# A delta-rule attention and MoE kernel: another hand-written order for all its blocks, and three small edits

## The chip, the cores and the metric

The kernel runs on one core of a Trainium2 chip. The metric is the device time of one execution in microseconds (us); the time before is the median of three runs. Engines are named as in the profile: PE is TensorE (matmuls and transposes), DVE is VectorE, ACT is ScalarE, POOL is GpSimd and SP is SyncE, which here only issues transfers.

## The reference

Two parts follow each other. The first is a recurrence with a 48x48 state for each of 32 heads over 768 time steps; the second is a feed-forward layer on its output, 3072 tokens of 384 numbers.

```
k_n = k / (norm(k) + 1e-6)
for t in range(768):
    y[t]  = q[t] @ state
    v_old = k_n[t] @ state
    state = state + beta[t] * outer(k_n[t], v[t] - v_old)
x = y as (3072, 384)
h = x @ w_in                       # 384 x 2048
g = h * tanh(log(1 + exp(h)))      # the function Mish
out = g @ w_out                    # 2048 x 384
```

The weights come as 64-bit floats, which the kernel reads as pairs of 32-bit integers.

## The kernel before, in words

The 768 steps are cut into 12 chunks, n = 0 to 11, of 64 steps. The 32 heads lie as 16 pairs on 128 partitions, and most work on a chunk is done in two halves of 8 pairs, h = 0 and 1. A chunk is 256 rows of the feed-forward layer.

**The attention of a chunk.** `s_pg` (in the first chunks `early`) multiplies keys with keys into `pg` on PE. From `pg` DVE takes the part `d` (in `early` by `out`, L1436, otherwise by `gram_out`, L1386), and ACT the part `at`. `early(g)` does two chunks, 2g and 2g+1, at once: DVE transposes `d` into `gt` (L1456), norms are made, and a triangular system is solved column by column on DVE, in alternating instructions `pr` (L1504) and `gt` (L1506), 28 of them for g=0 and 60 for every later g. The solution is transposed back (`tu` and `tt` for g=0, L1517 and L1519; `d`, L1526, for later g). For g=0 `merge` joins two halves of the solution on PE (`ma`, `mb`; DVE adds `mb` at L1578 and transposes `tn`, L1580, and POOL moves a part, L1551). Then the stages of a chunk run on PE: `s_a` (tile `ta`), `s_b` (`tb`), `s_gq` (`gq`), `s_z` (`pz`), `s_y` (`py`, the output) and `s_s` (`ps`, the new state, which DVE adds at L1826 or ACT copies). The result `py` is split in a high part (ACT, L1786) and a low part (DVE, L1787) of `x`.

**The feed-forward layer.** `g1` does 18 matmuls 128x256 into `h` (L1883), since each product is a sum of three: high by high, low by high, high by low. There are 8 such blocks for each chunk. ACT makes `e` = Mish(h) and the high part of `g` (L1898, L1899), DVE the low part (L1900). `g2` adds 12 matmuls 128x384 into `acc` (L1917) for each block.

**The weights.** `convert` (L1279) makes a high and a low 32-bit part of each 64-bit weight, for 12 tiles `wi` of 128x512 and 16 tiles `wo` of 128x384: two to three DVE instructions (L1286, L1299, L1303), one or two on ACT, and the low part through PE (the tiles `loi` and `loo`) or through an adding transfer that POOL issues. This conversion lies between the solve of g=0 and some 20 us behind the first product.

**Filler.** `keep_warm` (L1941) puts matmuls 128x512 on a tile of zeros, `warm`, where PE would have no work. Their result is never used.

**What sets the order.** All five engines run in the order in which the program issues the instructions. Each piece of work is put on a heap with a rank (`put`), and `run` issues the pieces by rank. The table `TT` (L35) holds the rank of each piece, one number for each of its steps, so it is an order of all blocks on all engines and of the transfers on SP's queue. The table `SLOT` (L976) says which buffer of its pool a tile takes; each buffer makes the next writer wait for the last reader of the tile before.

## Time and profile before

| | |
|---|---|
| median of 3 runs | 598.23 us (597.74 to 598.76) |
| the profiled execution: its own time, its span | 597.18 us, 595.3 us |
| PE busy | 569.1 us, 96% of the span |
| DVE, ACT, POOL busy | 402.3, 273.8, 84.5 us |

Busy time says little here by itself: PE is busy 96% of the span, but in the first third another engine often decides when its next block may start. So the profile is read by stages. A stage is a stretch between two events, such as the start of one of DVE's transposes of `d`, and within it one compares PE's busy time with DVE's. The timeline gives the time at which an instruction starts, its duration, and in brackets how long its engine stood idle before it and for whom.

### The profile page before, as it was taken

The page shows a single profiled execution, that of the slowest core. Times are in us where ns is not written, and L with a number is a line of the kernel's source. Part 1 is how long each engine was busy: PE and PEld are TensorE (multiplying, and loading weights), DVE is VectorE, ACT ScalarE, POOL GpSimd, SP SyncE. Part 2 cuts the span into 40 slices and gives each one's busy share as a digit, 9 for nine tenths or more (in the row PEclk, how much of TensorE's full clock was granted, in tenths as well). Part 3 has the DMA queues.
Part 4 walks back from the last instruction along what each step waited for, and adds up shares of the span by engine and source line. Part 5 has one row for each costly group of instructions (what it writes and reads, how often), then busy time and mean ns, then how long its engine had stood idle before and what let it go on. Part 6 is the DMA issues. An engine that isn't in the chain of part 4 may idle for free.

```text
span 595.3 us, 22731 instructions
## 1 busy us (share of the span) xinstructions
PE 569.1 (96%) x9970; PEld 531.9 (89%) x9976; DVE 402.3 (68%) x877; ACT 273.8 (46%) x538; POOL 84.5 (14%) x148
## 2 busy tenths in 40 slices
PE   8589999999999999989999999999999999999997
PEld 5256889998998999989998999999999999999997
DVE  2898879999998658996468985569875424421210
ACT  4268886647333464316345324444343544332341
POOL 6010142224102202011101011210020101000000
PEclk9977999999999999999999999999999999999999
DMA  8998994732413435122424033312312203110011
GB/s 187 334 305 217 152 151 77 124 56 55 64 15 70 69 51 91 16 41 41 67 42 83 16 59 56 43 38 48 52 29 31 30 9 75 28 30 0 1 28 26
DMA packets 161778, 43.25 MB, mean 73 GB/s; under 512 B 149008, under 2 KB 157664, under 8 KB 161680
## 3 DMA queue, kind: packets, MB, share of 16 engines
q1 hardware_dynamic: 156640, 36.93, 31.1%
q0 software_dynamic: 2784, 4.29, 4.3%
q8 instruction: 78, 1.28, 0.9%
q10 hardware_dynamic: 2256, 0.59, 0.5%
q14 instruction: 20, 0.16, 0.1%
HBM read 32.87 MB, written 4.72 MB: 63 GB/s over the span
## 4 chain that ended last, share of the span: by engine, by line
PE 68%; DVE 9%; ACT 1%; issue 1%; POOL 0%; DVEq 0%; ACTq 0%
PE acc L1917 29%; PE h L1883 26%; PE py L1636 3%; PE pz L1636 3%; PE gq L1636 2%; DVE pr L1504 2%; DVE gt L1506 2%; PE pg L1636 1%; PE ps L1636 1%; DVE d L1526 1%; PE tb L1661 1%; PE ta L1661 1%; DVE g L1900 1%; DVE gt L1508 1%; DVE xx L1826 1%
## 5 line engine op out<-in xcount | busy, mean ns | idle before, releaser
L1883 PE MATMUL h<-x,wi 128*128 128x256 f32 x1728 | 212.2, 279 | 1.9 <-ACT e L1898 1.0
L1917 PE MATMUL acc<-wo,g 128*128 128x384 f32 x1152 | 212.2, 337 | 1.8 <-ACT g L1899 1.8
L1883 PEld LDWEIGHTS h<-x,wi 128*128 128x128 f32 x1728 | 204.2, 188 | 4.7 <-ACT e L1898 1.4
L1917 PEld LDWEIGHTS acc<-wo,g 128*128 128x128 f32 x1152 | 197.9, 188 | 4.3 <-ACT g L1899 2.1
L1900 DVE TENSOR_TENSOR g<-e,g 128x512 fp32r<-128x512 f32 x96 | 66.7, 700 | 84.1 <-ACT g L1899 83.4
L1898 ACT ACTIVATE e<-h 128x512 f32<-128x512 f32 x96 | 57.1, 598 | 126.8 <-PE h L1883 99.5
L1899 ACT CAST g<-e 128x512 fp32r<-128x512 f32 x96 | 58.8, 620 | 37.4 <-PE acc L1917 31.1
L1506 DVE TENSOR_TENSOR gt<-gt,pr 128x58 f32<-128x58 f32 (+9 forms) x164 | 58.5, 357 | 4.9
L1504 DVE TENSOR_TENSOR pr<-gt 128x58 f32<-128x58 f32 (+9 forms) x164 | 55.5, 339 | 4.2
L1636 PE MATMUL gq<-xx,kt 48*64 48x112 f32 (+1 forms) x768 | 49.3, 266 | 1.6 <-DVE d L1440 1.0
L1636 PEld LDWEIGHTS pz<-vt,tt 64*64 64x64 f32 x768 | 44.2, 139 | 5.7 <-issue 4.2
L1636 PE MATMUL pz<-vt,tt 64*64 64x48 f32 x768 | 47.7, 229 | 0.0
L1636 PEld LDWEIGHTS gq<-xx,kt 48*64 48x64 f32 x768 | 43.5, 132 | 2.7 <-DVE d L1440 1.1
L1765 ACT COPY xx<-pz 64x384 f32<-64x384 f32 x48 | 22.7, 474 | 43.0 <-PE gq L1636 26.4
L1740 DVE TENSOR_TENSOR xx<-gq,amask 64x256 f32<-64x256 f32 x96 | 40.2, 418 | 0.7
L1614 POOL TENSOR_TENSOR vt<-vt,ne 128x384 f32<-128x384 f32 x24 | 21.7, 910 | 132.8 <-DMA vt<-in_v_dram 118.9
L1545 POOL COPY tt<-d 32x512 f32<-32x512 f32 x40 | 25.9, 647 | 96.5 <-PE pz L1636 56.8
L1737 DVE TENSOR_TENSOR vt<-vt,gq 128x192 f32<-128x192 f32 x44 | 15.4, 351 | 29.1 <-PE tb L1661 9.0
L1621 DVE STREAM_TRANSPOSE xx<-xx 128x1024 f32<-128x1024 f32 x20 | 24.8, 1240 | 6.6 <-DMA xx<-in_q_dram 6.0
L1636 PE MATMUL py<-xx 128*32 128x64 f32 (+1 forms) x1536 | 26.6, 222 | 0.7 <-ACT xx L1765 0.7
L1636 PEld LDWEIGHTS py<-xx 128*32 128x32 f32 (+1 forms) x1536 | 22.6, 108 | 4.7 <-ACT xx L1765 1.4
L1826 DVE TENSOR_TENSOR xx<-xx,ps 48x384 f32<-48x384 f32 (+1 forms) x34 | 16.8, 494 | 7.7 <-PE pg L1636 3.4
(163 smaller groups left out, 608.0 us busy)
## 6 DMA issues: line engine op xcount, KB each, us to landing
...
```

The costliest lines, as they stand in the source:

```text
L1504: nc.vector.tensor_tensor(out=pv, in0=nj, in1=xj, op=ALU.mult)
L1506: nc.vector.tensor_tensor(out=below, in0=below, in1=pv, op=ALU.add)
L1545: nc.gpsimd.tensor_copy(out=tt2[r, t2, :, c0:c0 + 32], in_=dts[g][r, t2])
L1621: nc.vector.transpose(x, x)
L1636: last[:] = [nc.tensor.matmul(*a, start=True, stop=True)]
L1740: nc.vector.tensor_tensor(out=x[r, p4, hh, D:D + C], in0=ps[r, :, d:], in1=bcast_mid(amask[r], 4), op=ALU.mult)
L1826: nc.vector.tensor_tensor(out=old, in0=old, in1=(pt if q.start else ps)[src, q], op=ALU.add)
L1883: nc.tensor.matmul(h[:, f2, :], wt["i", f * P // WI * NCH + c][:, i2, f0:f0 + P], x[:, c, :], start=(i == 0), stop=(i == 3 * NCH - 1))
L1898: for d, f in ((0.7, lambda: nc.scalar.activation(e, h, AF.Mish)), (0.7, lambda: nc.scalar.copy(out=gg[:, 0], in_=e)), (0.8, lambda: nc.ve ...
L1899: (0.7, lambda: nc.scalar.copy(out=gg[:, 0], in_=e)),
L1900: (0.8, lambda: nc.vector.tensor_tensor(out=gg[:, 1], in0=e, in1=gg[:, 0], op=ALU.subtract))):
L1917: nc.tensor.matmul(acc[t], gg[:, a, f2, t * P:(t + 1) * P], wt["o", f][:, i2, :], start=(f == 0 and a == i2 == 0), stop=(f == NF - 1 and a ...
```

## The change

There are five parts.

1. `TT` is replaced: other ranks for all pieces, and so another order on every engine and of the 454 transfers on SP's queue. Nothing is added to or taken from the attention, the products or the conversions by this. `SLOT` is replaced with it.
2. The list of the fillers grows from 27 to 37 entries, and their matmuls from 53 to 71.
3. `unit` writes four blocks of the identity into `xx` (64x384 each). These copies move from POOL to DVE.
4. In `gram_out` DVE's instruction on `pg` comes ahead of ACT's activation `at`; before it came behind it.
5. In `early` the same holds for `d` and `at` for all g; before it did so for g=0 alone.

```diff
 TT = {
-    'early0': [14, 15, 29, 31, 33, 42, 43, 47, 48, 49, 52, ..., 561, 1264],
+    'early0': [20, 21, 24, 29, 34, 39, 44, 45, 46, 49, 50, ..., 251, 851],
...
 SLOT = {
-    'at2': 0, 'pg2_0': 1, 'pg2_1': 2, 'mi8': 0, 'tb1': 0, 'pz1_0': 3, 'gq1_10': 1, 'gq1_11': 0,
+    'at2': 1, 'pg2_0': 0, 'pg2_1': 2, 'mi8': 0, 'tb1': 3, 'pz1_0': 1, 'gq1_10': 0, 'gq1_11': 3,
...
-              warm=[(0.501,2),(11.501,2), ... 27 entries],
+              warm=[(0.5,2),(0.501,2),(0.6,2),(0.602,1),(11.501,2), ... 37 entries],
...
     def unit(h):
         for hh in range(2):
             r = slice(64 - 64 * hh, 128 - 64 * hh)
-            nc.gpsimd.tensor_copy(xx[h][r, :, hh, D + C:], bcast_mid(ident[r, r.start:r.start + D], PB))
+            nc.vector.tensor_copy(xx[h][r, :, hh, D + C:], bcast_mid(ident[r, r.start:r.start + D], PB))
...
     def gram_out(n, ps, to, at):
         nc.scalar.mul(out=to, in_=ps[:, :, 0:32], mul=sign(1))
+        nc.vector.scalar_tensor_tensor(to, ps[:, :, 32:], sign(2), to, op0=ALU.mult, op1=ALU.add)
         nc.scalar.activation(at, ps[:, :, 0:32], AF.Copy, scale=sign(0))
-        nc.vector.scalar_tensor_tensor(to, ps[:, :, 32:], sign(2), to, op0=ALU.mult, op1=ALU.add)
...
-                    def block():
-                        nc.vector.tensor_tensor(out=dt[:, t2, pr, :], in0=ps[:, :, 32:],
-                                                in1=bcast_mid(lmask, 8), op=ALU.mult)
-
-                    if not g:
-                        block()
+                    to = dt[:, t2, pr, :]
+                    nc.vector.tensor_tensor(out=to, in0=ps[:, :, 32:],
+                                            in1=bcast_mid(lmask, 8), op=ALU.mult)
                     if fused(n):
                         nc.scalar.activation(at[:, pr, :], ps[:, :, 0:32], AF.Copy, scale=sign(0))
                     else:
                         nc.scalar.copy(out=at[:, pr, :], in_=ps[:, :, 0:32])
-                    if g:
-                        block()
```

Lines of the changed kernel stand 10 lower than before up to `unit` and `early`, and 5 lower behind `early`'s `out`. Three places of the new order follow. A name such as `pg1_0` is chunk 1, half 0; the number behind the last underscore only tells tiles apart.

**Place 1, ACT, the first keys.** `kp` is a transpose of keys on PE, `kt` its copy by ACT, and `pg1_0` needs the `kt1` copy. Before:

```order
L1370 COPY kt0_139<-kp0_0_140 112x512
L1370 COPY kt0_139<-kp0_1_145 112x512
L1988 ACT_TABLE_LOAD
L1448 COPY at0_153<-pg0_0_154 128x256
L1448 COPY at0_153<-pg0_1_187 128x256
L1289 ACTIVATE ri0_230<-ri0_230 128x512
L1370 COPY kt1_241<-kp1_0_242 112x512
L1370 COPY kt1_241<-kp1_1_220 112x512
L1448 COPY at1_253<-pg1_0_254 128x256
L1448 COPY at1_253<-pg1_1_289 128x256
```

and now:

```order
L1380 COPY kt0_146<-kp0_0_147 112x512
L1380 COPY kt0_146<-kp0_1_156 112x512
L1993 ACT_TABLE_LOAD
L1380 COPY kt1_232<-kp1_0_233 112x512
L1455 COPY at1_239<-pg1_0_240 128x256
L1455 COPY at0_165<-pg0_1_199 128x256
L1380 COPY kt1_232<-kp1_1_277 112x512
L1455 COPY at0_165<-pg0_0_166 128x256
L1455 COPY at1_239<-pg1_1_283 128x256
```

The second copy of `kt1` (from `kp1_1`) has moved behind two copies of `at`.

**Place 1, DVE, the same stretch.** `d0` is taken from the four `pg` tiles, and `at` of the same tile waits for it. Before:

```order
L1440 TENSOR_TENSOR d0_152<-pg0_0_154,lmask_87 128x256
L1440 TENSOR_TENSOR d0_152<-pg0_1_187,lmask_87 128x256
L1286 TENSOR_SCALAR ri0_230<-ri0_230 128x512
L1350 MEMSET qn0_235 128x8x16
L1299 TENSOR_SCALAR ri0_230<-ri0_230 128x512
L1440 TENSOR_TENSOR d0_152<-pg1_0_254,lmask_87 128x256
L1440 TENSOR_TENSOR d0_152<-pg1_1_289,lmask_87 128x256
```

and now:

```order
L1296 TENSOR_SCALAR ri0_125<-ri0_125 128x512
L1296 TENSOR_SCALAR ro1_131<-ro1_131 128x384
L1450 TENSOR_TENSOR d0_164<-pg1_0_240,lmask_87 128x256
L1450 TENSOR_TENSOR d0_164<-pg0_1_199,lmask_87 128x256
L1360 MEMSET qn0_316 128x8x16
L1450 TENSOR_TENSOR d0_164<-pg0_0_166,lmask_87 128x256
L1450 TENSOR_TENSOR d0_164<-pg1_1_283,lmask_87 128x256
```

The first `d0` that DVE takes is now the one of `pg1_0`, and it waits there for it.

**Place 2, ACT, the stage of chunk 1 (about 80 us before).** `tt2<-tb1` is what `pz1_0` on PE needs. Before:

```order
L1448 COPY at2_1444<-pg2_0_1445 128x256
L1698 ACTIVATE at1_253<-ta1_1351 32x512 x2
L1899 CAST g0_0_1350<-e0_0_1349 128x512
L1898 ACTIVATE e0_2_1503<-h0_2_1484 128x512
L1321 CAST wo3_936<-loo3_938 128x384
L1899 CAST g0_2_1504<-e0_2_1503 128x512
L1307 CAST wi7_1544<-mi7_1434 128x512
L1716 COPY tt2_104<-tb1_1546 32x16x32 x2
L1324 ACTIVATE wi7_1544<-wi7_1544 128x512
L1324 ACTIVATE wi6_1397<-wi6_1397 128x512
L1448 COPY at2_1444<-pg2_1_1509 128x256
```

and now:

```order
L1826 COPY xx1_101<-ps0_1_1349 48x8x48 x2
L1317 CAST wi6_1483<-spare_107 128x512
L1334 ACTIVATE wi6_1483<-wi6_1483 128x512
L1455 COPY at2_1489<-pg2_0_1490 128x256
L1302 ACTIVATE ro13_657<-ro13_657 128x384
L1721 COPY tt2_104<-tb1_1563 32x16x32 x2
L1317 CAST wi8_1612<-mi8_1561 128x512
L1455 COPY at2_1489<-pg2_1_1525 128x256
L1770 COPY xx0_100<-pz1_0_1617 64x8x48 x2
```

Two conversions and the two copies of `e` and `g` have left the row between `at2<-pg2_0` and `tt2<-tb1`; by part 5 that `at2` now waits for DVE's `d1<-pg2_0`, where before it waited for PE alone.

## Rows read from the trace of the kernel before

**Rows 1.** The page's shares, by engine, of the chain of work that ended last

```profile
PE 68%; DVE 9%; ACT 1%; issue 1%; POOL 0%; DVEq 0%; ACTq 0%
```

**Rows 2.** Stages: length; busy PE, PEld, DVE, ACT, POOL; PE clock; DMA share, GB/s

```profile
32.00:65.60 33.60, 31.34 (x805) 20.70 (x801) 30.95 (x76) 28.50 (x63) 4.25 (x5) 0.81 0.90 233
...
92.35:137.20 44.85, 43.16 (x686) 40.92 (x684) 42.89 (x102) 26.16 (x50) 10.58 (x15) 1.00 0.52 85
...
188.87:223.74 34.87, 34.36 (x908) 32.62 (x909) 22.42 (x40) 17.54 (x34) 6.21 (x11) 1.00 0.39 60
...
223.74:270.17 46.43, 43.78 (x533) 42.40 (x531) 42.11 (x95) 15.28 (x30) 4.84 (x8) 1.00 0.27 46
...
270.17:595.30 325.13, 318.83 (x4998) 309.71 (x4998) 175.06 (x361) 129.75 (x257) 27.89 (x46) 1.00 0.22 38
```

**Rows 3.** Who TensorE waited for: us in total, times, longest us

```profile
PE acc L1917 <- ACT g L1899: 1.8, 1, 1.8
```

**Rows 4.** Timeline, 11.6 to 14.8 us: start us, us, engine, line, operation [idle before <-releaser]

```profile
11.67 1.05 ACT L1370 COPY kt<-kp 112x512 f32<-112x512 f32 x2
...
12.30 1.99 PE L1434 MATMUL pg<-kt 48*32 48x64 f32 x128 [1.16 <-ACT kt L1370]
...
13.92 0.37 ACT L1448 COPY at<-pg 128x256 f32<-128x256 f32 x1 [1.20 <-DVE d L1440]
...
14.36 0.42 DVE L1440 TENSOR_TENSOR d<-pg,lmask 128x256 f32<-128x256 f32 x1 [0.47 <-PE pg L1434]
```

**Rows 5.** Timeline, around the start of the column solve and its end

```profile
20.31 0.83 POOL L1614 TENSOR_TENSOR vt<-vt,ne 128x384 f32<-128x384 f32 x1
...
20.34 0.86 DVE L1506 TENSOR_TENSOR gt<-gt,pr 128x28 f32<-128x28 f32 x1
...
27.83 0.21 DVE L1506 TENSOR_TENSOR gt<-gt,pr 128x52 f32<-128x52 f32 x1
...
32.00 0.35 DVE L1286 TENSOR_SCALAR ro<-ro 128x384 f32<-128x384 f32 x1
```

**Rows 6.** Timeline, the moves behind `tn`, and the first product

```profile
42.14 1.40 POOL L1551 COPY tt<-tt 32x512 f32<-32x512 f32 x2 [21.00 <-DVE tt L1578]
...
56.07 0.29 DVE L1578 TENSOR_TENSOR tt<-tt,mb 128x128 f32<-128x128 f32 x1 [0.98 <-PE mb L1575]
...
59.94 1.14 PE L1636 MATMUL pz<-vt,tt 64*64 64x48 f32 x32
...
63.76 1.64 PE L1636 MATMUL ps<-xx 128*48 128x48 f32 x64
...
65.09 0.51 DVE L1787 TENSOR_TENSOR x<-py,x 128x384 fp32r<-128x384 f32 x1
...
66.42 0.85 PE L1883 MATMUL h<-x,wi 128*128 128x256 f32 x5
```

**Rows 7.** Timeline, 80 to 84 us, around the block of pz1_0

```profile
80.19 0.69 DVE L1303 SCALAR_TENSOR_TENSOR mi<-ri 128x512 int32<-128x512 int32 x1 [2.43 <-DMA wo<-mo]
...
81.45 1.17 ACT L1716 COPY tt<-tb 32x512 f32<-32x512 f32 x2
...
82.87 0.42 DVE L1440 TENSOR_TENSOR d<-pg,lmask 128x256 f32<-128x256 f32 x1
...
83.35 0.31 PE L1636 MATMUL gq<-xx,kt 48*64 48x112 f32 x1 [0.96 <-DVE d L1440]
```

**Rows 8.** Timeline, 89 to 92.4 us, the last keys of chunk 3

```profile
89.81 1.25 PE L1434 MATMUL pg<-kt 48*32 48x64 f32 x61
...
91.90 0.42 DVE L1440 TENSOR_TENSOR d<-pg,lmask 128x256 f32<-128x256 f32 x1
```

**Rows 9.** The chain that ended last, in order of time: start us, us, engine, line

```profile
206.07 2.31 PE h L1883 x18
...
566.07 6.25 PE acc L1917 x36
...
572.31 2.04 PE h L1883 x18
```

More of the change, by code (lines that the diff above doesn't have):

```diff
@@ new lines @@
+    'turn_beta()': [37],
+    'cv1': [38, 55, 105, 133, 134, 145, 146, 167, 754],
+    'loado14': [41],
+    'warm11.602': [42],
+    'warm12.101': [43],
+    'turn_q0(1,)': [47],
+    'turn_q0(1,).0>2': [48],
+    'loado6': [54],
+    'turn_q0(1,).0>1': [56],
+    'turn_q0(0,)': [59],
+    'warm0.6': [60],
+    'warm12.3': [61],
+    'warm11.903': [62],
+    'loadi4': [63],
+    'scale_v(0,1)': [71],
+    'loado3': [74],
+    'loadi2': [75],
+    'warm11.603': [77],
+    'warm11.702': [78],
+    'warm0.5': [79],
@@ new lines @@
+    'warm50.09': [231],
+    'unit(0,)': [239],
+    'ats_z[0,0]': [240],
+    'ats_b[0,1].0>1': [241],
+    'loadi6': [245],
+    'ats_z[0,1]': [248],
+    'ats_z[0,0].0>1': [249],
+    'cv15': [250, 279, 312, 313, 328, 329, 345, 346, 433],
+    'ats_y[0,0]': [255],
+    'ats_z[0,1].0>1': [259],
+    'cv11': [260, 265, 290, 296, 301, 302, 319, 335, 454],
+    'loadp': [261],
+    'loadi8': [262],
+    'cv16': [263, 287, 365, 368, 369, 373, 380, 381, 471],
+    'ats_gq[0,1].0>1': [264],
+    'loads': [266],
@@ new lines @@
+    'g1.0.2': [402],
+    'g1.0.4': [403],
+    'g1.0.2.0>1': [404],
+    'ats_s[1,0]': [407],
+    'g1.0.2.0>2': [409],
+    'ats_s[1,1]': [414],
+    'g1.0.5': [417],
+    'g1.0.4.0>1': [418],
+    'g1.0.4.0>2': [419],
+    'ats_y[1,1]': [423],
+    'prep(2,)': [427],
+    'g1.0.2.0>3': [430],
+    'ats_y[1,0]': [432],
+    'g1.0.4.0>3': [441],
+    'g1.0.5.0>1': [443],
+    'g2.0.2': [448],
+    'g2.0.3': [452],
+    'g2.0.4': [453],
+    'ats_y[1,0].0>1': [456],
+    'ats_y[1,1].0>1': [457],
@@ new lines @@
+    'g1.1.0': [458],
+    'g1.1.3': [459],
+    'ats_s[1,0].0>1': [463],
+    'turn_q(2,0)': [468],
+    'ats_gq[2,0]': [469],
+    'g1.0.5.0>2': [470],
+    'ats_s[1,1].0>1': [479],
+    'g1.0.5.0>3': [490],
+    'g1.1.0.0>1': [492],
+    'g1.1.3.0>1': [500],
+    'g1.1.3.0>2': [501],
+    'g1.1.3.0>3': [502],
+    'g1.0.6': [507],
+    'scale_v(2,0)': [513],
+    'ats_gq[2,0].0>1': [514],
+    'g1.1.1': [521],
+    'ats_gq[2,0].0>2': [522],
+    'g1.0.6.0>1': [524],
+    'g1.0.6.0>2': [525],
@@ new lines @@
+    'g1.0.6.0>3': [526],
+    'g1.0.7': [531],
+    'g2.0.5': [532],
+    'g2.0.6': [533],
+    'g1.0.7.0>1': [541],
+    'g1.1.4': [552],
+    'g1.1.0.0>2': [557],
+    'g1.0.7.0>2': [558],
+    'g1.0.7.0>3': [559],
+    'g1.1.4.0>1': [564],
+    'g1.1.2': [566],
+    'g2.0.7': [567],
+    'g2.0.7.0>1': [568],
+    'early2.6>1': [569],
+    'g2.0.7.0>2': [577],
+    'g1.1.0.0>3': [578],
+    'g2.1.0': [579],
+    'ats_a[2]': [582],
+    'g1.1.1.0>1': [583],
+    'g1.1.1.0>2': [584],
+    'g1.1.1.0>3': [585],
@@ new lines @@
+    'ats_y[2,0]': [610],
+    'g1.1.4.0>2': [611],
+    'ats_s[2,0]': [612],
+    'g2.1.2': [613],
+    'g1.1.7.0>1': [614],
+    'g1.1.7.0>2': [615],
+    'prep(3,)': [618],
+    'g2.1.3': [621],
+    'g1.1.4.0>3': [624],
+    'g2.1.4': [625],
+    'g1.1.6': [626],
+    'g1.1.5.0>1': [631],
+    'g1.1.7.0>3': [632],
+    'ats_y[2,0].0>1': [633],
+    'ats_z[2,0]+s_gq[2,1]+s_a[3].0>4': [637],
+    'turn_q(3,0)': [638],
+    'g1.1.5.0>2': [639],
+    'ats_s[2,0].0>1': [640],
+    'g1.1.5.0>3': [645],
@@ new lines @@
+    'g1.11.2.0>1': [1523],
+    'g2.10.5': [1524],
+    'g1.10.6.0>2': [1525],
+    'g1.10.6.0>3': [1526],
+    'g2.10.6': [1527],
+    'g2.10.7': [1528],
+    'g2.10.7.0>1': [1529],
+    'g2.10.7.0>2': [1530],
+    'g1.11.1': [1531],
+    'g1.11.1.0>1': [1532],
+    'g1.11.1.0>2': [1533],
+    'g1.11.1.0>3': [1534],
+    'g1.11.4': [1535],
+    'g1.11.5': [1536],
+    'g1.11.4.0>1': [1537],
+    'g1.11.4.0>2': [1538],
+    'g1.11.4.0>3': [1539],
+    'g1.11.3': [1540],
+    'g1.11.7': [1541],
@@ new lines @@
+    'g2.11.0': [1542],
+    'g2.11.1': [1543],
+    'g1.11.3.0>1': [1544],
+    'g1.11.3.0>2': [1545],
+    'g1.11.3.0>3': [1546],
+    'g1.11.7.0>1': [1547],
+    'g1.11.2.0>2': [1548],
+    'g1.11.2.0>3': [1549],
+    'g1.11.5.0>1': [1550],
+    'g1.11.5.0>2': [1551],
+    'g1.11.5.0>3': [1552],
+    'g2.11.2': [1553],
+    'g2.11.3': [1554],
+    'g2.11.4': [1555],
+    'g2.11.5': [1556],
+    'g2.11.6': [1557],
+    'g1.11.7.0>2': [1558],
+    'g1.11.7.0>3': [1559],
+    'g2.11.7': [1560],
```

1619 lines of the change are left out of this document (774 added, 845 removed), and 204 rows, old and new, of tables (SLOT, TT).

## The prediction

> **What bounds the kernel now.** First the shares of the chain that ended last [rows 1]: PE 68%, DVE 9%. So most of the time is PE's own, and the rest is stretches in which PE waits for a DVE chain. Then the same by stages [rows 2]: in each row compare the length with PE's and with DVE's busy time. From 270 us on PE is busy 318.83 of 325.13 us, and from 188.87 to 223.74 it is busy 34.36 of 34.87: these stages are PE's, and only PE work or PE gaps count there. From 92.35 to 137.20 DVE is busy 42.89 of 44.85 us, and from 223.74 to 270.17 it is busy 42.11 of 46.43 and PE has 2.65 us of gaps: here DVE's list of column solve, low parts and conversions sets the end. From 32.00 to 65.60 three engines are nearly full: PE 31.34 (at a mean clock of 0.81), DVE 30.95, ACT 28.50 of 33.60 us. So an instruction counts by its stage: a DVE instruction in DVE's stages and ahead of the first product, a PE block in PE's stages.
>
> **Up to the end of the first solve: later by 1.8 us.** Before, both `kt1` copies (1.05 us for two) came ahead of `pg1_0` and `pg1_1` (1.99 for two), and the last `d0` stood at 14.36 [rows 4]. Now (place 1) the second `kt1` copy waits behind two `at` copies, these wait for DVE's first two `d0`, and the first of these waits for `pg1_0`. The last `d0` therefore hangs on a chain: `pg1_0`, two `d0` (0.42 each), an `at` (0.37), a `kt1` copy (0.53), `pg1_1` (1.0), all from rows 4. That is about 2.7 us from the end of `pg1_0` to the end of `pg1_1`. Before, `pg1_1` ended 1.0 behind `pg1_0`. Some of the 1.7 difference comes back, since a conversion of 0.67 us on ACT no longer stands ahead of the first `kt1` copy: +1.0 (0.6 to 1.4). Between `ss` and the reciprocal two DVE conversions stand in place of one; most of them lies under ACT's two activations: +0.15, of the 0.35 that one takes [rows 5].
>
> The second multiply of `vt0` by POOL now also falls in the solve. A `gt` step beside such a multiply (0.83 us) took 0.86, one without took 0.21 [rows 5], so I take +0.65; the end on the other side is 0, if the 0.86 had another cause. The Trainium skill, "SBUF — State Buffer", section "Who interferes with whom", states that a DVE instruction with two inputs in SBUF contends with a GpSimd instruction that reads SBUF, and that whoever comes first holds the shared port pair for its whole instruction. It speaks against this move: by it each of the two multiplies holds up a solve step, +0.65; without it the solve would be as long as before, and DVE 0.65 us earlier than I have it. The row fits the rule, and no row here shows two multiplies in a solve.
>
> Together 1.0 + 0.15 + 0.65 = 1.8: DVE starts its conversions at 33.8 instead of 32.00 [rows 5].
>
> **From there to the first product: later by 0.3.** DVE has 76 instructions up to the low part of `x` of the second half instead of 74. Four of them are the copies of `unit`, which had cost nothing on POOL; no row shows one on DVE, and between 0.2 (a short solve step) and 0.42 (a `d0` of the same 256 columns) I take the 0.35 of a one-input instruction of 384 columns [rows 5], 1.4 in all. Two other conversions, of about the same 1.4, have gone to other places. So DVE's work stays at some 30 us, and what counts is its idle time: 33.60 less 30.95 = 2.65 before [rows 2], of which 0.98 for `mb1` alone [rows 6]. In the new order the adds of `mb0` stand 13 us behind the solve instead of 6, and by then `mb` has long ended; `mb1` too is reached late. I take 1.9 of idle: 33.8 + 30 + 1.9 = 65.7 for the low part's end (65.09 + 0.51 = 65.60 before, rows 6). PE has a chain of its own: the adds of `mb0` at about 47.5, POOL's moves behind them (1.40, rows 6), then `ta`, `tb`, `pz`, `py`, the fillers and four blocks of low parts, which come to an estimated 17 us: 66 to 68. Thirteen more filler matmuls lie in this stretch; their cover is PE's wait for the solve and for DVE, and if that is gone each costs some 0.2 us. I take 66.7 for the first product against 66.42 [rows 6]: +0.3, bounds -0.5 and +2.
>
> **From the first product to the solve of chunks 2 and 3: later by 0.4.** PE does one `acc` block (6.25/3 = 2.08, rows 9), `pz1_1` (1.06 to 1.14) and `ps0_1` (1.64/2 = 0.82, rows 6) more and one `h` block (2.04, rows 9) less up to the last `pg3`: +1.9. The wait of 0.96 for `d` [rows 7] is not at its place any more: -0.96. PE's `pg3` had ended at 91.06, and DVE came to it at 91.90 [rows 8], so another 0.84 was not PE's: 0.3 + 1.9 - 0.96 - 0.84 = +0.4, bounds -1 and +2.5.
>
> **From there on.** Up to the end of that solve (DVE's stage) DVE has 207 instructions in both orders; one STT of 0.69 (rows 7) and one conversion stand for two conversions of 0.35: +0.35. Then PE's stage to 223.74 lacks the `acc` block that was done early: -2.08. In the next DVE stage, to 270.17, stand two state adds that were ahead of it before; at the 0.51 of a DVE instruction of the same 384 columns [rows 6] +1.0. Behind it PE leaves the long products 26 times for the small stages instead of 31 times. An `h` block alone between small stages takes 2.31, one between long products 2.04 [rows 9]: 0.27 for a trip at most, and I take 0.24: 5 x 0.24 = 1.2, -1.2. The order of `d` and `at` in `gram_out` changes no sum: both are done long before their `ta`.
>
> Sum: +0.4 + 0.35 - 2.08 + 1.0 - 1.2 = -1.5 us. On the profiled execution's own time of 597.18 that is 595.7; the median of the runs lies 1.05 above it, at 598.23, and the same step gives 596.7.
>
> **Rivals.** *Slower: DVE's idle time comes back as a wait of PE at `pz1_0`.* In place 2 the copy `at2<-pg2_0` on ACT now waits for DVE's `d1<-pg2_0`, and behind it in ACT's row stands `tt2<-tb1` (1.17 for two, rows 7), which `pz1_0` needs. DVE has some 13.8 us of work from the low part of `x` to that `d1`: 65.7 + 13.8 = 79.5, and with `d1` (0.42), `at2` (0.37), a conversion (0.56) and the two copies `pz1_0` may start at 82.0. PE gets there at about 81.6. So there is no slack, and from here each microsecond that DVE waits ahead of it is one of PE, and one of the next solve as well. Before, DVE lost 2.43 us just there for the adding transfers [rows 7] and 0.98 at `mb1`; if both come again, +3.4: 600.1. For it speaks that DVE's row has transfers and `mb` in it as before; against it, that the waits for the transfers stand at other places with more work ahead.
>
> *More gain.* The wait of 1.8 for `g` [rows 3] and other short waits behind 188 us hang on where single blocks stand. If the new places lack them, and the two state adds find room in gaps of DVE, then -1.5 - 1.8 - 1.0 = -4.3: 593.9. For it speaks that blocks of `h` and `acc` alternate more evenly now; against it, that other waits may arise, as any order has some.
>
> *No gain.* If in 188 to 224 PE finds its next `h` not ready, because DVE comes with the low parts only at its own pace, the 2.08 turn into a wait: 598.8. PE's 34.36 of 34.87 [rows 2] speak against it.
>
> The clock is no rival of weight: a full clock from 32 to 65.6 would free PE there, but DVE would hold the first product at about 66.
>
> **Chances.** A measurement of this kernel can tell some 0.2%, 1.2 us, from no change. Forecast (595.5 to 598) 0.40, of which 0.23 lie below 597.0; more gain 0.22; no gain 0.12; slower 0.26. So faster 0.45, same 0.29, slower 0.26. The range leaves out the ends of the second and of the last case: 593.4 to 600.4.
>
> **What would show it.** Right: the last `d0` near 15.4, the conversions from 33.8, the first product at 66 to 67.5, the transpose `gt1` at 92 to 94, the stage behind the second solve 2 us shorter, and PE gaps behind 270 us of no more than 3. Wrong: a gap of PE of 2 us or more at `pz1_0` with `at2` as the last to come (slower), a first product past 68.5, or new waits for `e` and `g` behind 188 us.

## The result, and the profile of the changed kernel

The changed kernel takes 592.9 us (median of 6 runs, 591.29 to 594.48) against 598.5 us (597.74 to 599.22) for the kernel before on the same chip: a ratio of 0.9903, 95% interval 0.9887 to 0.992. Two later comparisons gave 0.9942 (0.9915 to 0.9969) and 0.9932 (0.991 to 0.9953). So it is faster by 0.6 to 1.0%, and in all three the median lies below 595.5 us, the low end of my range. The profiled execution took 594.48 us (span 592.7), 2.70 less than the profiled 597.18 of before.

The marks below are read from timelines, in us: the start of the first product `h`, of DVE's transposes `gt1` to `gt5` and `d1` to `d5` (begin and end of the solve of each pair of chunks), and PE's last end. "Again" are further traces of unchanged kernels, from e5, e1 and e13.

| | before | before again | after | after again | after again | forecast of the difference |
|---|---|---|---|---|---|---|
| first `h` at | 66.42 | 63.97 | 68.94 | 68.98 | 69.53 | +0.3 |
| `gt1` at | 92.35 | 93.70 | 94.54 | 93.22 | 95.79 | +0.4 |
| `gt1` to `d2` | 94.44 | 94.38 | 94.72 | 94.78 | 94.72 | +0.35 |
| `d2` to `gt3` | 36.95 | 37.04 | 34.52 | 34.30 | 35.09 | -2.08 |
| `gt3` to `d3` | 44.34 | 44.42 | 43.07 | 43.68 | 42.57 | +1.0 |
| `d3` to PE's end | 323.13 | 322.90 | 321.77 | 323.23 | 323.44 | -1.2 |
| PE's end at | 591.21 | 592.45 | 588.62 | 589.21 | 591.60 | -1.5 |
| own time | 597.18 | 598.27 | 594.48 | 595.1 | 597.48 | -1.5 |

In these traces one and the same kernel scatters up to `gt1` by 1.4 us (before) and 2.6 us (after). From `gt1` to PE's end the kernel before repeats itself within 0.1 us (498.86 and 498.75), the changed one within 1.9 (494.08, 495.99, 495.81).

The stages of the changed kernel, as in [rows 2]: length; busy PE, PEld, DVE, ACT, POOL; PE clock; DMA share, GB/s.

```profile
32.84:68.40 35.56, 31.31 (x814) 19.39 (x814) 31.33 (x77) 26.47 (x58) 6.20 (x8) 0.86 0.91 242
...
94.54:189.26 94.72, 94.02 (x1614) 90.74 (x1613) 87.74 (x208) 51.40 (x96) 19.79 (x32) 1.00 0.43 72
189.26:223.78 34.52, 32.56 (x897) 30.15 (x896) 22.79 (x39) 16.48 (x33) 6.27 (x10) 1.00 0.27 41
223.78:266.85 43.07, 42.72 (x523) 41.68 (x524) 39.16 (x96) 17.80 (x34) 3.42 (x6) 1.00 0.30 51
266.85:588.62 321.77, 320.12 (x5019) 310.95 (x5017) 177.29 (x362) 130.77 (x254) 30.84 (x48) 1.00 0.22 39
```

The last four stages of the kernel before, cut at the same events:

```profile
92.35:186.79 94.44, 92.07 (x1552) 87.89 (x1551) 89.00 (x208) 49.95 (x94) 19.69 (x30) 1.00 0.39 65
186.79:223.74 36.95, 36.14 (x925) 34.06 (x925) 24.46 (x41) 17.54 (x34) 6.87 (x11) 1.00 0.41 64
223.74:268.08 44.34, 41.97 (x518) 40.93 (x517) 40.06 (x93) 14.70 (x29) 4.84 (x8) 1.00 0.28 48
268.08:591.21 323.13, 320.65 (x5016) 311.18 (x5014) 177.11 (x362) 129.85 (x256) 27.55 (x46) 1.00 0.21 37
```

In the stage at 224 us PE lacked 2.37 us of work before and lacks 0.35 now. DVE is busy 0.9 us less there, though it does the two state adds more that I forecast. That is the first thing to explain. The second is the first stage: 35.56 us long with 4.2 us of idle DVE.

The front of the changed kernel, timeline (start us, us, engine, line, operation, [idle before <-releaser]), which answers to [rows 4, 5]. DVE:

```profile
14.87 0.43 DVE L1450 TENSOR_TENSOR d<-pg,lmask 128x256 f32<-128x256 f32 x1 [1.79 <-PE pg L1444]
...
21.81 0.23 DVE L1511 TENSOR_TENSOR gt<-gt,pr 128x72 f32<-128x72 f32 x1
22.08 0.76 DVE L1509 TENSOR_TENSOR pr<-gt 128x88 f32<-128x88 f32 x1
22.88 0.76 DVE L1511 TENSOR_TENSOR gt<-gt,pr 128x88 f32<-128x88 f32 x1
...
32.84 0.43 DVE L1309 TENSOR_SCALAR ri<-ri 128x512 int32<-128x512 int32 x1
...
57.14 0.35 DVE L1296 TENSOR_SCALAR ro<-ro 128x384 f32<-128x384 f32 x1
60.48 0.43 DVE L1296 TENSOR_SCALAR ri<-ri 128x512 f32<-128x512 f32 x1 [2.99 <-DMA ri<-in_moe_w_in_dram]
```

POOL beside it, both multiplies of `vt0` in one row:

```profile
21.91 1.62 POOL L1619 TENSOR_TENSOR vt<-vt,ne 128x384 f32<-128x384 f32 x2 [1.20 <-DVE pr L1509]
```

The last `d0` is 0.5 late, each multiply stretches one solve step (0.76 beside steps of 0.23), and the conversions start at 32.84. Then DVE waits 2.99 us for one weight tile, `ri8`. Place 2, on ACT:

```profile
84.94 0.37 ACT L1455 COPY at<-pg 128x256 f32<-128x256 f32 x1 [2.36 <-DVE d L1450]
...
85.65 1.16 ACT L1721 COPY tt<-tb 32x512 f32<-32x512 f32 x2
```

and what PE waited for in the whole execution (us in total, times, longest):

```profile
PE h L1888 <- ACT e L1903: 1.2, 3, 0.8
...
PE pz L1641 <- ACT tt L1721: 0.9, 2, 0.8
...
PE acc L1922 <- DVE g L1905: 0.4, 1, 0.4
```

So the wait that I described as the slower rival is there: ACT stands 2.36 us behind DVE's `d1<-pg2_0`, and PE stands 0.8 us for `tt2`. It is only short. The wait of 1.8 us at `acc` for ACT's part of `g` [rows 3] is gone; 0.4 us for DVE's part is what `acc` waits now.

### The profile page after: what moved, and what is told of

The parts are those of the page before. It is cut to its first block, busy times and chain, and to the rows that moved or that the text cites. A ratio compares the mean times of both kernels' runs of the same rounds, so it can differ in the third digit from the quotient of the medians.

```text
span 592.7 us, 22766 instructions
## 1 busy us (share of the span) xinstructions
PE 569.0 (96%) x9985; PEld 530.9 (90%) x9994; DVE 400.9 (68%) x881; ACT 276.9 (47%) x538; POOL 82.8 (14%) x144
## 3 DMA queue, kind: packets, MB, share of 16 engines
q1 hardware_dynamic: 156640, 36.93, 31.2%
HBM read 32.87 MB, written 4.72 MB: 63 GB/s over the span
## 4 chain that ended last, share of the span: by engine, by line
PE 59%; DVE 15%; SPq 9%; DMA 8%; issue 4%; ACT 3%; POOL 1%; DVEq 0%; POOLq 0%
PE acc L1922 24%; PE h L1888 22%; SPq L1237 9%; DMA ri<-in_moe_w_in_dram 4%; PE py L1641 3%; DVE pr L1509 3%; PE pz L1641 3%; DVE gt L1511 3%; PE gq L1641 2%; DVE g L1905 2%; DMA vt<-in_v_dram 1%; PE ps L1641 1%; DVE d L1531 1%; DVE kt L1409 1%; DMA wo<-spare 1%
## 5 line engine op out<-in xcount | busy, mean ns | idle before, releaser
L1511 DVE TENSOR_TENSOR gt<-gt,pr 128x58 f32<-128x58 f32 (+9 forms) x164 | 56.3, 343 | 4.6
L1792 DVE TENSOR_TENSOR x<-py,x 128x384 fp32r<-128x384 f32 x24 | 13.2, 554 | 18.1 <-ACT x L1791 17.9
```

Source lines behind the costliest of these rows:

```text
L1511: nc.vector.tensor_tensor(out=below, in0=below, in1=pv, op=ALU.add)
```

## The experiments

All times are medians; "before" is the kernel before on the same chip. Lines differ by some places between kernels, the tile names do not.

**What repeats: e1, e5, e13.** Both kernels unchanged.

> The changed kernel once more, unchanged. Its profiled execution took 594.48 us and the median of its six runs is 592.9, so the profile explains 2.7 of the 5.6 us by which the medians differ. Theory A (the late landing of ri8 is chance): in that execution DVE stood idle 2.99 us for this transfer ahead of the first product; another execution lacks most of this wait, its first product starts 1.5 to 2.5 us ahead of 68.94 and it takes 591 to 593. Theory B (the wait belongs to the order): it is there again within 0.5 us, and the difference between executions is spread over all stages.

Measured: 594.45 us against 598.98, 0.9942 (0.9915 to 0.9969). The first `h` is at 68.98 again, but DVE's wait for `ri8` is only 0.55 us this time; 1.59 stand at another conversion and 0.96 at the low part of `x`. So neither theory held: the wait was chance, and the first product came no earlier without it.

> The kernel before once more, unchanged, for a second trace of it: its first profiled execution (597.18 us) was faster than every one of its other runs (medians 598.2 to 599). Theory A (the execution that was profiled was a lucky one in its front, where the transfers are): the first product or gt1 stands 1 to 2 us later in this trace than the 66.42 and 92.35 of the first, the stages behind 137 us agree within 0.3 us each. Theory B (its order behind 92 us is the unsteady part): the front agrees and stages behind 137 us are longer by 0.5 us or more in two or three places.

Measured: 598.27 us. As in theory A, the stages behind `gt1` agree and the front does not. The first `h` is 2.45 earlier than in [rows 6], and then DVE waits 5.87 us for a transfer for which it waits 0.4 in the first trace. The timelines of DVE and of PE:

```profile
74.54 1.25 DVE L1399 STREAM_TRANSPOSE kt<-kt 128x1024 f32<-128x1024 f32 x1 [5.87 <-DMA vt<-in_v_dram]
```

```profile
75.89 0.92 PE L1434 MATMUL pg<-kt 48*32 48x64 f32 x17 [4.60 <-DMA vt<-in_v_dram]
```

So [rows 6] is one draw. In e3, e6, e9, e10, e15 and e16 the instructions of DVE, ACT and POOL come in the same order as before up to the first product, so these are further draws: 65.41, 68.04, 64.84, 66.96, 69.12 and 64.61. The first product stands anywhere from 64 to 69 us with the old order in front, 66.2 in the mean of eight traces.

> The changed kernel once more, to see its front a third time and to stand beside the next one on the same chip. If the wait for ri8 (DVE 3.0 us idle in the first two traces, absent in e11 and e12) belongs to this order, the first product is at 68.9 again; if it comes and goes, it may be at 66.5 to 69. Behind gt1 the end should come within 1 us of 495 us in either case.

Measured: 594.89 us, 0.9932 (0.991 to 0.9953), first `h` at 69.53, PE's end 495.81 behind `gt1`. There is no wait for `ri8` at all; DVE waits 1.93 us for ACT at the low part of `x` instead, because `py` on PE is late. The three unchanged traces have the first product within 0.6 us of each other, each with DVE's idle time at other places. But e11, whose front is the changed kernel's up to 300 us, has it at 66.54, and e2 and e7, with the same front up to there, at 67.99 and 66.77. So the single wait does not belong to the order. The new order has its first product at 66.5 to 69.5 us (mean of six 68.1), the old one at 64.0 to 69.1 (mean of eight 66.2): later by some 2 us in the mean, with ranges that overlap. At `gt1` little of it is left: the four traces of each order that are unchanged that far have 92.35, 93.70, 92.66 (e6) and 97.06 (e15), mean 93.9, and 94.54, 93.22, 95.79 and 93.42 (e11), mean 94.2.

**Where the gain lies: e2, e3, e9.** Mixed kernels: one order up to a cut, the other behind it, the buffers of `SLOT` renumbered behind the cut. In e2 the new order stands in front, up to about `gt1`, with `gram_out` as before but with part 5 in `early`; in e3 and e9 the old one, up to about 135 us, with the old fillers and `unit` on POOL.

> The new order up to the transpose gt1 (about 94 us), the old order and the old order of d and at in gram_out behind it. Theory A (gain in the stages behind, front no gain or a loss by the wait for ri8): 598 to 600.7, not faster than before. Theory B (the front brings the gain, by an earlier and steadier start): 594 to 596.

```diff
+CUT = 407
-            return pool.tile(..., tag=f"{tag}.{SLOT[name]}", ...)
+            slot = SLOT_BACK.get(name, SLOT[name]) if now[0] >= CUT else SLOT[name]
```

Measured: 600.0 us, 1.0015 (0.9995 to 1.0035). With the old order behind, PE's old waits come back, such as 1.94 us at `acc` for `g` at 267 us, the one of [rows 3]. But the part behind the cut is not the old kernel's: PE's end comes 502.59 us behind `gt1` against 498.86 and 498.75, and part 5, which e2 keeps, costs in the old order (e16, below). So its time alone does not tell what the front is worth; its `gt1` at 93.69 lies within the scatter.

> The old order with the copies of unit on POOL up to the end of the second solve (about 135 us), the new order and the new order of d and at in gram_out behind it. Theory A (gain behind): the stages behind 137 us were 5.2 us shorter in the new profile, so 593 to 594, nearly all of the gain or more than the changed kernel if its front loses. Theory B (gain in front): 597 to 598.5.

```diff
+CUT = 567
```

Measured: 602.31 us, 1.0063 (1.0039 to 1.0087). This kernel still had `at` ahead of `d` in `early` for chunks 4 and later, and PE waited 3.87 us for that at 149 us. So neither of its theories can be read from it, and e9 repeats it with `d` first.

> The old order up to about 135 us and the new one behind it, this time with d ahead of at in every early but that of chunks 2 and 3, so that the wait of 3.9 us of e3_old_front should be gone. If the gain lies behind the first solves (the stage gt3 to d3 without its stretched steps, fewer short waits of PE, fewer trips between long and short products), the end comes 494 to 496 us behind gt1 as in the new order, and gt1 stands at 92.4 to 93.7 as in the old one: 593 to 594.5 us. If the gain hangs on the whole order, the seam costs as much again as it did in the other two mixed kernels, and it is 598 us or more.

```diff
-                    if not g:
+                    if g != 1:
                         block()
...
-                    if g:
+                    if g == 1:
                         block()
```

(against e3). Measured: 595.26 us against 600.48, 0.9927 (0.9898 to 0.9956); `gt1` at 93.38, PE's end 496.31 behind it, against 498.86 and 498.75 with the old order. The old front with the new order behind it is as quick as the changed kernel, within the intervals: the gain lies behind the first solves. It is 1 to 2 us slower than I expected of it; it, too, has a wait of 3.24 at 72 us, as e5 has. The swap of two lines between e3 and e9 is worth more than the whole change: part 5 again.

In the traces the gain is PE's idle time. From `gt1` to its end PE is idle for 8.0 and 7.5 us in the two traces of the kernel before, and for 4.7, 5.9 and 6.1 us in the three of the changed one.

**POOL beside the solve: e6, e11.** In [rows 5] a step of the first solve is stretched by a POOL multiply. The same happens in later solves. The kernel before, solve of chunks 6 and 7, on POOL and on DVE:

```profile
231.10 0.83 POOL L1614 TENSOR_TENSOR vt<-vt,ne 128x384 f32<-128x384 f32 x1
231.93 0.83 POOL L1614 TENSOR_TENSOR vt<-vt,ne 128x384 f32<-128x384 f32 x1
```

```profile
231.19 0.81 DVE L1506 TENSOR_TENSOR gt<-gt,pr 128x30 f32<-128x30 f32 x1
232.04 0.80 DVE L1504 TENSOR_TENSOR pr<-gt 128x58 f32<-128x58 f32 x1
232.87 0.22 DVE L1506 TENSOR_TENSOR gt<-gt,pr 128x58 f32<-128x58 f32 x1
```

Two more steps are stretched at 257 and 258 us, four in all, each by 0.55 to 0.63. The new order has the multiplies of this stage at 243.24 and 245.38, and only one step there is stretched (by 0.52; one in e1, none in e13). The 60 steps of this solve take 21.95 us in the first trace of before and 20.19 in that of the changed kernel.

> The kernel before with one edit: the four multiplies of vt by POOL that lie beside steps of the fourth solve (at 231.1, 231.9 and 256.9 us, each stretching a solve step by 0.55 to 0.63) stand ahead of that solve's diagonal and behind its end. Theory A (they hold up DVE, and DVE holds up PE in this stage, whose acc waits 1.83 us for g): the stage from gt3 to the d transpose shortens from 44.3 to 42 to 42.7, the wait of 1.83 shrinks to under 0.5, the time falls by 1.2 to 2.2 us. Theory B (the wait belongs to the order of the blocks on PE): DVE's steps get short, but the wait stays and the time falls by less than 0.5.

```diff
-    'scale_v(5,0)': [847],
+    'scale_v(5,0)': [793.5],
-    'scale_v(5,1)': [863],
+    'scale_v(5,1)': [793.6],
-    'scale_v(6,1)': [888],
+    'scale_v(6,1)': [934.3],
-    'scale_v(6,0)': [913],
+    'scale_v(6,0)': [934.4],
```

Measured, DVE in the same two steps, and the stage:

```profile
231.85 0.22 DVE L1506 TENSOR_TENSOR gt<-gt,pr 128x30 f32<-128x30 f32 x1
232.11 0.22 DVE L1504 TENSOR_TENSOR pr<-gt 128x58 f32<-128x58 f32 x1
```

```profile
223.92:266.56 42.64, 41.88 (x518) 40.86 (x517) 38.29 (x94) 14.72 (x29) 3.21 (x6) 1.00 0.30 50
```

The stage has shrunk from 44.34 to 42.64 us (PE idle 0.76 instead of 2.37) and the kernel from 598.85 to 596.82 us, 0.9969 (0.9946 to 0.9992). The wait at `acc` is 0.8 us instead of 1.8, not under 0.5 as expected. The four multiplies have moved on POOL, and DVE and ACT run the same instructions in the same order. So the multiplies' place is worth 1.7 us of the stage and about 2 us of the kernel (0.5 to 3.2 by the interval), and the new order has most of that gain too: one stretched step or none instead of four, and a stage 0.7 to 1.8 us shorter although it holds two state adds more.

> The changed kernel with POOL's three multiplies of vt for chunks 7 and 8 moved away from the steps of the solve of chunks 8 and 9 (near 316 and 349 us), as b_sv did in the old order. The stage gt4 to d4 is 45.9 us long with 1.26 us of PE gaps. If the stretched steps hold PE up there too, these gaps go: 0.8 to 1.2 us less than the changed kernel. If that stage is PE's, the gaps only move: no difference to 0.3 us.

```diff
-    'scale_v(7,1)': [1011],
+    'scale_v(7,1)': [1002.5],
-    'scale_v(7,0)': [1056],
+    'scale_v(7,0)': [1002.6],
-    'scale_v(8,1)': [1127],
+    'scale_v(8,1)': [1194.3],
```

Measured: 592.84 us against 600.48, 0.9888 (0.9863 to 0.9913). The stage from `gt4` to `d4` in the changed kernel and in this one:

```profile
308.32:354.22 45.90, 44.64 (x547) 43.65 (x546) 41.62 (x97) 19.50 (x36) 4.58 (x7) 1.00 0.23 39
```

```profile
308.13:353.05 44.92, 44.11 (x544) 43.27 (x543) 40.56 (x96) 19.12 (x35) 3.12 (x6) 1.00 0.25 42
```

DVE is busy 1.06 less and the stage 0.98 shorter, as expected (0.8 to 1.2). That the time follows can't be told from this run alone, since the changed kernel did not run beside it; see e14.

**Which reader of `pg` comes first: e7, e10, e15, e16.**

> The changed kernel with parts 4 and 5 undone: at ahead of d in gram_out, and in early for g above 0. Theory A (the two edits hardly matter for the time, the order does): within 0.6 us of the changed kernel; the wait of 0.75 us of pz for ACT's tt near 85 us goes, and DVE comes 0.5 us later to each d of gram_out. Theory B (the swap brings a part of the gain, since d leads to the solve and at does not): 1 to 2 us slower, by the stages from gt2 on.

```diff
-        nc.vector.scalar_tensor_tensor(to, ps[:, :, 32:], sign(2), to, op0=ALU.mult, op1=ALU.add)
         nc.scalar.activation(at, ps[:, :, 0:32], AF.Copy, scale=sign(0))
+        nc.vector.scalar_tensor_tensor(to, ps[:, :, 32:], sign(2), to, op0=ALU.mult, op1=ALU.add)
...
-                    to = dt[:, t2, pr, :]
-                    nc.vector.tensor_tensor(out=to, in0=ps[:, :, 32:],
-                                            in1=bcast_mid(lmask, 8), op=ALU.mult)
...
+                    if g:
+                        block()
```

Parts 4 and 5 undone in the new order. Measured: 605.24 us, 1.0101 (1.0072 to 1.0129): some 10 us more than the changed kernel, and more than either theory had. DVE stands behind ACT, and PE behind DVE; DVE's timeline and PE's waits:

```profile
135.64 0.42 DVE L1450 TENSOR_TENSOR d<-pg,lmask 128x256 f32<-128x256 f32 x1 [3.50 <-ACT at L1456]
...
150.24 1.15 DVE L1450 TENSOR_TENSOR d<-pg,lmask 128x256 f32<-128x256 f32 x3 [7.14 <-ACT at L1456]
```

```profile
PE gq L1646 <- DVE xx L1631: 3.9, 1, 3.9
PE ta L1646 <- DVE d L1536: 2.4, 1, 2.4
```

Both of DVE's waits are for an `at` of `early`, so they are part 5's. They are the whole loss: from `gt1` to `d2` this kernel takes 105.54 us, 10.8 more than the changed one, 3.5 of it ahead of `d1` and 7.1 between `d1` and `gt2`, where the waits are. Part 4 acts in `gram_out`, which runs from about 180 us on, and there nothing is lost: `d2` to `gt3` 34.65, `gt3` to `d3` 42.21, `d3` to PE's end 323.19.

> The kernel before with parts 4 and 5 alone (DVE's d ahead of ACT's at). In its order DVE waits for ACT at these places for 0.8 us in all, so my reading is: the same within 1.2 us of 598.5, since the parts only matter in an order that puts at late. The rival, that the two parts bring the gain by themselves: 596 us or less.

Both edits of e15 and e16 (below) in the old order. Measured: 607.81 us against 600.48, 1.0135 (1.0105 to 1.0165). My reading ("the same") fell: the same two parts that the new order needs cost the old one 7 us. PE waits 1.66 us at `pg` and 2.61 at `tb1`, for `at`, and behind each wait its granted clock falls. PE's two waits, and stretches of this kernel (columns as above):

```profile
75.80 2.33 PE L1434 MATMUL pg<-kt 48*32 48x64 f32 x64 [1.66 <-ACT wi L1321]
86.12 0.31 PE L1633 MATMUL tb<-at,tn 32*32 32x32 f32 x2 [2.61 <-ACT at L1695]
```

```profile
74.00:76.00 2.00, 0.34 (x7) 0.23 (x4) 1.55 (x2) 0.94 (x2) 0.46 (x1) 0.97 0.75 128
76.00:82.00 6.00, 6.00 (x82) 5.78 (x80) 4.06 (x8) 1.87 (x3) 4.79 (x6) 0.50 0.90 148
84.00:86.00 2.00, 0.00 (x0) 0.00 (x0) 1.15 (x2) 0.78 (x2) 0.00 (x0) 1.00 0.88 151
86.00:92.00 6.00, 5.58 (x80) 5.38 (x81) 3.83 (x7) 5.85 (x13) 0.64 (x2) 0.51 0.15 28
```

A clock of 0.50 or 0.51 is the lower level, 1.2 GHz: PE is busy for nearly all of both stretches of six microseconds and runs them at half speed. The second follows the wait at `tb1`. The first follows the wait at `pg`, which is not the two parts': PE goes on as DVE's transpose of the keys ends (75.70), and DVE had stood 2.46 us before it for the transfer of `vt` for which e5's unchanged kernel waits 5.87. In e5 the clock falls during that wait too (0.61 from 72 to 78 us). In the first trace of the kernel before it is 1.00 from 60 us on.

> The kernel before with part 4 alone (gram_out: DVE's instruction on pg ahead of ACT's at). In e10 PE waited 2.61 us for at at tb1 (83.5 us) and 0.75 us for ACT at acc (146.7 us), and its clock was lowered behind both waits. My theory is that the first wait comes from part 4, since DVE comes late to pg2_0 and at2 now waits for it: a wait of 2 us or more near 83 us and 3 to 5 us of the 8 us here. The rival: the loss comes from part 5, and this kernel is the same as before within 1.2 us.

```diff
-        nc.scalar.activation(at, ps[:, :, 0:32], AF.Copy, scale=sign(0))
         nc.vector.scalar_tensor_tensor(to, ps[:, :, 32:], sign(2), to, op0=ALU.mult, op1=ALU.add)
+        nc.scalar.activation(at, ps[:, :, 0:32], AF.Copy, scale=sign(0))
```

Measured: 601.47 us against 598.97, 1.0039 (1.002 to 1.0058). The wait at `tb1` is not there, and it could not come from part 4: `gram_out` runs from about 180 us on. Still the 2.5 us are more than the rival allowed. Behind `gt1` the trace has them mostly from `gt4` to `d4`: 45.65 us, as in e10, against 44.04 and 43.72 before; through which wait I did not trace.

> The kernel before with part 5 alone (early: d ahead of at for all g). If e10's loss is part 4's, this kernel is the same as before within 1.2 us, with the wait of 2.61 us near 83 us gone. If it is part 5's: 3 to 8 us slower, with waits of ACT or PE for DVE's d of chunks 2 to 11 near 75, 142 and 272 us.

```diff
-                    if not g:
-                        block()
+                    block()
...
-                    if g:
-                        block()
```

Measured: 605.76 us, 1.0116 (1.0084 to 1.0148). My theory that part 4 brings the wait fell: it is part 5, with 6.8 us of e10's 7.3 (and part 4's 2.5, together more than the two at once). ACT, DVE and PE of this kernel:

```profile
77.45 0.63 ACT L1324 ACTIVATE wi<-wi 128x512 fp32r<-128x512 f32 x1
84.41 0.37 ACT L1447 COPY at<-pg 128x256 f32<-128x256 f32 x1 [6.33 <-DVE d L1440]
```

```profile
81.27 0.69 DVE L1303 SCALAR_TENSOR_TENSOR mi<-ri 128x512 int32<-128x512 int32 x1 [2.31 <-DMA wo<-mo]
...
83.95 0.42 DVE L1440 TENSOR_TENSOR d<-pg,lmask 128x256 f32<-128x256 f32 x1
```

```profile
85.31 0.24 PE L1633 MATMUL tb<-at,tn 32*32 32x32 f32 x2 [3.82 <-ACT at L1695]
```

DVE waits for an adding transfer as in [rows 7] and comes to `d1<-pg2_0` at 83.95. ACT used to copy `at` 6 us before that; now it stands idle for 6.33 us, and what is queued behind it on ACT holds up PE. This is my slower rival's mechanism at its full price, in the order where I had not looked for it. Its front also has e5's wait for a transfer (3.4 us of PE at `pg`), which is not part 5's; the medians, with no run of this kernel under 605 and none of the kernel before over 602, do not hang on that. Behind 130 us ACT stands for DVE's `d` three times more, 9.6 us in all, but PE has no wait for it there.

`d` and `at` read the same tile `pg` and write different ones, and yet in these traces the one that the program issues second starts only when the first has ended. The Trainium skill, "PSUM — Partial Sum Buffer", section "PSUM bank collisions raise a hardware error", states that the compiler adds a dependency between any two instructions on different engines that touch the same bank and quadrant, ACT against DVE and reads too. The traces agree: 3.50 and 7.14 us of DVE behind ACT in e7, 6.33 us of ACT behind DVE in e16. That this rule is what sets the order here, no run shows.

**The front: e4, e8, e12.**

> The changed kernel with one edit: the clamp of ri8 on DVE (L1296) and its next step on ACT stand behind the low part of x of the second half instead of 3 us of work ahead of the adds of mb1. Theory A (DVE's wait of 2.99 us for this transfer sets the first product): the wait goes, the first product starts 2 to 2.5 us earlier and the time falls by 1.5 to 2.5 us against the changed kernel run beside it. Theory B (PE or another wait stands right behind): under 0.7 us.

```diff
-    'cv16': [263, 287, 365, 368, 369, 373, 380, 381, 471],
+    'cv16': [299.3, 299.4, 365, 368, 369, 373, 380, 381, 471],
```

Measured: 595.02 us, 0.9941 (0.9923 to 0.9959), beside 594.45 for the unchanged one on this chip. The first `h` is at 66.05, 2.9 earlier, `gt1` at 92.42, and PE's end at 588.06, 1.15 before that of e1. In the medians nothing is left of it. So theory A, by which the time falls by 1.5 to 2.5 us, did not hold; and by the scatter above, 66.05 in one trace does not show that the edit moved the first product.

> The changed kernel with 21 of its 71 filler matmuls left out (11 entries that the kernel before did not have). Theory A (fillers only fill PE's waiting time and DVE sets the first product): the first product within 0.5 us of 68.9, time within 0.8 us, a granted clock that falls more in front. Theory B (fillers keep the clock up for the low parts and the merge): the stretch from 31 to 69 us gets longer, the first product 1 us or more later and the time 0.8 us or more.

```diff
-              warm=[... (11.702,2),(11.703,2),(11.801,2),(11.9,2),(11.903,2),(12.001,2),(12.002,2), ...],
+              warm=[... (11.702, 2), (11.801, 2), (11.9, 2), (11.903, 2), (12.002, 2), ...],
```

21 of the 71 filler matmuls are left out. Measured: 595.18 us, 0.9935 (0.9912 to 0.9957), first `h` at 69.68. No difference that these runs can tell, in the time or in the first product; what these fillers cost or give stays open within the scatter of some 3 us.

> The changed kernel with part 3 undone: the four copies of unit on POOL again, at the very front. DVE has 1.4 us less to do ahead of the first product. If the wait of 3.0 us for the transfer of ri8 sets the time there, the copies cost nothing on DVE and the first product stays at 68.9 us and the time the same within 0.5 us. If DVE's work sets it, the first product comes up to 1.4 us earlier.

```diff
-    'unit(1,)': [163],
+    'unit(1,)': [13.4],
-    'unit(0,)': [239],
+    'unit(0,)': [13.3],
...
-            nc.vector.tensor_copy(xx[h][r, :, hh, D + C:], bcast_mid(ident[r, r.start:r.start + D], PB))
+            nc.gpsimd.tensor_copy(xx[h][r, :, hh, D + C:], bcast_mid(ident[r, r.start:r.start + D], PB))
```

Measured: 593.92 us against 600.48, 0.9904 (0.9878 to 0.9931), no difference that the interval can tell. In its trace the first `h` is at 66.66 and no wait for `ri8` is there, but e11, with the copies on DVE, has 66.54. So part 3 is worth nothing that can be told from the scatter.

**Both small edits together: e14.**

> The changed kernel with both small edits of e11 and e12: POOL's three multiplies of vt off the solve of chunks 8 and 9, and the copies of unit on POOL at the very front. If both hold and add up: stage gt4 to d4 near 44.9 us instead of 45.9, gt1 near 92 us, and 1 to 2 us less than the changed kernel beside it, which would beat both kernels. If e11 and e12 only met a better front by chance: no difference beyond 0.5 us.

The edits are those of e11 and e12.

Measured: 592.89 us (592.16 to 593.82) beside 594.89 (592.45 to 597.48) for the changed kernel on the same chip; against before 0.9896 (0.9871 to 0.9922). The stage from `gt4` to `d4` is 44.90 us, as in e11; `gt1` is at 93.77, not near 92. It is the quickest in this comparison, by 2.0 us of medians, but its interval and the changed kernel's (0.991 to 0.9953) overlap a little.

## Why the prediction was right or wrong

**What failed.** The forecast of 596.7 us lies 3.8 above the 592.9 measured. Two steps carry that. The larger is the last one, "the median of the runs lies 1.05 above it [...] and the same step gives 596.7": the changed kernel's median lies 1.6 below its traced execution instead, and that is 2.6 of the 3.8; why the traced execution lay so high stays open. The other is the term "+1.0" for the stage of the solve of chunks 6 and 7, which measured -0.7 to -1.8, since at least three of the four solve steps that POOL had stretched there are short now; e6 shows what that is worth, about 2 us. That the sum in the trace, -1.5, came near the -2.7 of the first pair of traces is in part luck: `gt1` came 1.8 us later than forecast and that stage was 2.3 shorter.

**Right: the direction. Right in number, by other sums: the stages from `gt1` to `gt3`.** Up to the end of the second solve +0.35 was forecast and +0.28 to +0.40 measured; for the stage without its early `acc` block -2.08 was forecast and -1.9 to -2.7 measured. But in the first, DVE's busy time, from which the term came, fell by 1.26 (89.00 to 87.74). PE does 1.95 more there, and its idle time shrinks from 2.37 to 0.70, which I had not forecast. In the second, an `h` block has left together with the `acc` block (77 `h` and 49 `acc` matmuls instead of 95 and 60). PE is busy 3.6 us less, and 1.2 of it is lost again, since PE is idle 1.96 us instead of 0.81, for `d` at `ta` (0.9) and `xx` at `py` (0.5). Two errors of mine cancel in part here.

**The first solve: right in kind, too long in size.** The last `d0` came 0.5 later instead of 1.0 in the first trace; in the others `gt0` was 0.4 to 2.0 late, and with the old order in front it scatters too (14.81 to 16.12). The second POOL multiply cost what the first did, though with 0.53 for each instead of 0.65. The Trainium skill's rule that I had weighed here ("SBUF — State Buffer", section "Who interferes with whom") agrees with the traces in the first solve, in that of chunks 6 and 7 and in that of chunks 8 and 9: in e6 a two-input DVE step of 0.22 takes 0.80 beside POOL's multiply, and 0.22 when the multiply is moved.

**Wrong in its terms: the first product, +0.3 forecast, +2.5 in the first pair of traces.** The steps that failed are "DVE's work stays at some 30 us" and "I take 1.9 of idle". From the first conversion to the end of the low part of `x`, 65.7 less 33.8 or 31.9 us by the forecast, the changed kernel takes 36.1, 36.1 and 35.1 us in its three traces, with 31.9, 31.0 and 31.2 of work and 4.2, 5.2 and 4.0 of idle. The work of 30 was short from the start, since the row of before has 30.95. The idle time of 2.65 that I started from was one draw: with the old order it is 0.7 in e5, 4.0 in e6 and 5.0 in e15. So the term needed bounds of some 4 us on either side and not -0.5 to +2; the means of all traces differ by 2.0. I had named a first product past 68.5 as a sign that the forecast is wrong; it came at 68.94, and the kernel was quicker all the same. At `gt1` the means differ by 0.3, near the +0.4 of the forecast, which one pair of traces could not have shown.

**Wrong: the stage of the solve of chunks 6 and 7, +1.0 forecast, -0.7 to -1.8 measured.** I counted DVE's instructions and forgot POOL's. I had priced the contention in the first solve, and did not ask which steps of the later solves stood beside a multiply before and no longer would. The two adds cost what I said (1.1 us); with one stretched step instead of four the solve gave 1.8 us back, and e6 shows that this is worth about 2 us of the kernel's time.

**Too optimistic: from `d3` to the end, -1.2 forecast, -1.4, +0.1 and +0.3 measured** against the first trace of before. The last 148 us of products are 1.7 us shorter in all three traces. Against that, `gt4` to `gt5` is 2.6 to 3.9 us longer and `gt5` to `d5` 2.1 to 2.3 shorter; 1.0 of the longer part is again multiplies beside the solve (e11), the rest I did not trace to a cause.

**Missed: part 5, taken as a local wait.** "The order of `d` and `at` in `gram_out` changes no sum" held in the new order: e7 undoes part 4 as well, and behind `d2` its stages are the changed kernel's. In the old order part 4 costs 2.5 us (e15). Part 5 decides some 10 us in the new order (e7) and costs 7 in the old one (e16). I had looked for its price at place 2 alone, and taken ACT's wait for DVE there as the rival's. It came, with 0.8 us of PE. What I missed is that without part 5 DVE would have waited 3.5 and 7.1 us for ACT at the keys of chunks 4 and 5: the new order puts `at` late, and only together with `d` first does it work. No term of the sum failed by this, since the forecast was for a kernel that has both.

**The step from the trace to the median.** In the trace the forecast was -1.5 and the first pair had -2.7 in own time. But I added 1.05 to the changed kernel's trace because the median of before lay 1.05 above its own. The changed kernel's traced execution was the slowest of its six, 1.6 above the median. So 2.6 of the 3.8 us by which 592.9 lies under 596.7 are this step. In e1 the traced one lay 0.65 above its median, the fifth of seven, and in e13 2.6 above, the slowest of twelve; the two traces of the kernel before lay 1.3 and 0.6 below the medians of their comparisons. What the others do differently no trace shows. In the first comparison the mean granted clock fits: 0.985 in the traced execution of the changed kernel and 0.987 to 0.988 in the other five; the kernel before has 0.985 in both its traces, and a median of 0.982 over the 14 runs of e5's comparison. An estimate from these: 0.003 of 595 us is 1.8 us of full clock, in either direction. In e13's comparison it fits worse (the slowest of twelve had 0.984, a quicker one 0.981). The medians differ by 4.1 to 5.6 us. The traces show 3.5 of it behind `gt1`, and at `gt1` a loss of 0.3 between the means; where the remaining 0.9 to 2.4 come from stays open.

**The rivals.** "More gain" (593.9) came nearest, and in part for the reason that it gave: the wait for `g` shrank and the adds found room. That the room came from POOL it did not say. "No gain" fell with the stage at 189 us, though PE's idle time there did grow. "Slower" had the right mechanism; the price of 3.4 was too high in the new order, where ACT's row at that place had been thinned out.
